# GpSimd makes one of four shifted exp copies and the normalising multiplications in place of VectorE

## The chip, the cores and the metric

The kernel runs on one NeuronCore of one Trainium2 chip. The metric is the time of one execution on the device, in microseconds (us). Executions of one kernel mostly agree within a per cent. "Faster" or "slower" needs a difference of over 2%.

The engines in the profile are PE (TensorE matmuls), PEld (TensorE weight loads), DVE (VectorE), ACT (ScalarE), POOL (GpSimd) and SP (SyncE, which issues DMAs here). The granted clock is the share of its full speed that TensorE was given, as the profile reports it. In the experiments a ratio compares the fast runs of one kernel with those of the kernel before in the same rounds, on the same chip; it is given as the measuring program recorded it, and is not quite the ratio of the medians that stand beside it.

## The reference

One transformer block: 2048 tokens, width 512, 32 heads of 16 columns, a gated FFN of width 1792, with shifts and scales made from a conditioning vector.

```python
h = layernorm(x) * (1 + ca) + sa
q, k, v = split(h @ wqkv)                       # 32 heads, Dh = 16
p = softmax(q @ k.T * Dh ** -0.5)
x = x + ga * ((p @ v) @ wo)
h = layernorm(x) * (1 + cb) + sb
x = x + gb * ((gelu(h @ w_gate) * (h @ w_up)) @ w_down)
```

What matters here: 32 x 2048 x 2048 scores have to go through an exponential. That is the dominant work of the kernel.

## The kernel before

A Python program decides the order of instructions on each engine, when the kernel is built, with a timing model of its own. Every engine then runs its list in order, and semaphores keep the dependences. All operations go through a few helpers, so a whole class of instructions shows one line in the profile: 309 is every matmul, 322 every ScalarE activation, 334 every `tensor_scalar`, 326 every `tensor_tensor`, 343 every copy.

Scores go to six PSUM banks in two groups of three. TensorE fills a group, ScalarE exponentiates it to bf16 in SBUF (`E`) while TensorE fills the other group. ScalarE cannot keep up with all blocks, so VectorE takes some. For a "quad" of four score blocks VectorE takes the third bank of the group, one block at a time, and writes an integer that is the bit pattern of a rough exponential:

```python
# (cut) in stream(): one step of the score loop
self.qk([(seq[m], k) for m, k in items])                       # TensorE: fill three banks
self.act(self.E[:, e0:e0 + n, :], self.scp[:, s0:s0 + n, :], ACT.Exp, scale=EXP_SCALE)
if g is not None:                                              # VectorE has the third bank
    j = quad["j"]
    kq = self.kq[quad["k"]]
    self.ts("dve", kq[:, 512 * j:512 * j + 512].bitcast(U16), self.scp[:, s0 + n, :], 128 / OCT, SHIFT_C,
            ALU.mult, ALU.add)
    ...
    if j == 3:
        quad["ready"].append((0, [kq[:, 512 * x:512 * x + 512] for x in range(4)]))
        for i in range(NS):                                    # NS = 4 shifted copies
            self.shift_task(quad, i)
```

One such block is too rough. The quad is multiplied with V, and four copies of it, each with a constant added to the bit pattern, with four scaled versions of V; the sum is accurate enough. Each copy is one instruction of 2048 columns of uint16, SBUF to SBUF, and one more group of matmuls reads it:

```python
def shift_task(self, q, i):
    def f():
        s = self.sq_free[0]
        self.ts("dve", self.sq[s].bitcast(U16), self.kq[q["k"]].bitcast(U16), float(SHIFT[i]), None, ALU.add)
        if self.probing is None:
            self.sq_free.pop(0)
            ...
            q["ready"].append((i + 1, [self.sq[s][:, 512 * x:512 * x + 512] for x in range(4)]))
    self.task([f], ("shift", q["rnd"][0]), lambda: bool(self.sq_free))
```

When a unit (eight of them make a set of query rows) is finished, its output is multiplied by reciprocals of the row sums, which come back from a round trip through DRAM:

```python
def fin2():
    c = OCOL[sets[0]]
    self.tt("dve", self.onorm[:, qd, c:c + W], osb, rb, ALU.mult)
```

The model of time that the scheduler uses has a line for GpSimd. `short(t)` in the same class inserts filler matmuls, whose results nobody reads, wherever the model finds TensorE idle and its recent activity below a mark (`FILL`).

```python
def cost(self, eng, out, ins, kind):
    ...
    if eng == "act":
        return n * 0.833 + (60 if ps else 92)
    if eng == "pool":
        return n * 3.0 + 100
```

The softmax here doesn't subtract the row's maximum and nothing guards it: scores larger than these inputs give would overflow.

## Time and profile before

| | before |
|---|---|
| time, median of 2 runs | 906.15 us (906.06 to 906.24) |
| span of the profiled run | 904.5 us |
| mean granted TensorE clock | 0.981 |
| busy, whole span: ScalarE / TensorE / VectorE / GpSimd | 841.9 / 817.2 / 687.5 / 3.7 us |

The first view is the table of stretches, for 102 to 780 us, which is from the first to the last shifted copy. Each engine's busy time is followed by its number of instructions in brackets; then come the granted clock, the DMA share and GB/s.

```profile
core 0: us, PE busy (x) PEld busy (x) DVE busy (x) ACT busy (x) POOL busy (x), PEclk, DMA share, GB/s
102.00:780.00 678.00, 638.02 (x9029) 199.85 (x9021) 570.82 (x996) 674.16 (x594) 0.00 (x0) 1.00 0.16 44
```

ScalarE is busy 674.2 of 678 us. It is the limit, and it is idle for 4 us. VectorE has 107 us of idle time there and GpSimd does nothing.

In the tile names, `dreg` and `mreg` are SBUF regions that hold quads and their copies, `ps_sc` is the banks of scores, `ps_pv` the bank of p @ v, which `osb` takes over, and `ps_mi` a bank for other products; `wreg` and `hreg` hold intermediate values of the FFN and other work. The groups of instructions, with shapes kept apart, give the price of each piece: columns are line, engine, operation, output<-input, shape, count | busy us, mean ns | idle us before, and who ended it.

```profile
L334 DVE TENSOR_SCALAR dreg<-ps_sc 128x512 uint16<-128x512 f32 x188 | 129.5, 690 | 36.0 <-PE ps_sc L309 34.0
L334 DVE TENSOR_SCALAR mreg<-dreg 128x2048 uint16<-128x2048 uint16 x188 | 123.1, 682 | 2.8 <-PE ps_pv L309 2.8
L334 DVE TENSOR_SCALAR mreg<-ps_sc 128x512 uint16<-128x512 f32 x92 | 63.0, 689 | 16.0 <-PE ps_sc L309 15.0
L334 DVE TENSOR_SCALAR mreg<-mreg 128x2048 uint16<-128x2048 uint16 x92 | 60.3, 684 | 0.9 <-PE ps_pv L309 0.9
L326 DVE TENSOR_TENSOR wreg<-wreg 128x1024 bf16<-128x1024 bf16 x42 | 28.3, 683 | 0.2
```

There are 188 + 92 = 280 evictions from PSUM at 690 ns, so 70 quads, and 280 copies at 683 ns. A copy handles four times as many columns as an eviction in the same time. The last line is a product of two SBUF tensors.

The waits of ScalarE and TensorE in the same stretch (engine and tile <- who ended the wait: us in total, times, longest us):

```profile
ACT E L322 <- PE ps_sc L309: 2.8, 9, 0.7
```
```profile
PE ps_sc L309 <- ACT E L322: 20.0, 61, 0.8
PE ps_mi L309 <- DVE wreg L339: 5.0, 8, 1.2
PE ps_mi L309 <- DVE wreg L343: 2.6, 5, 0.8
PE ps_mi L309 <- DVE kmo L334: 1.7, 5, 0.5
PE ps_pv L309 <- DVE mreg L334: 1.4, 6, 0.5
```

ScalarE almost never waits for scores. TensorE waits mostly for ScalarE to free a bank, which is as it should be with ScalarE as the limit.

### The profile page before, as it was taken

The page shows a single profiled execution, that of the slowest core. Times are in us where ns is not written, and L with a number is a line of the kernel's source. Part 1 is how long each engine was busy: PE and PEld are TensorE (multiplying, and loading weights), DVE is VectorE, ACT ScalarE, POOL GpSimd, SP SyncE. Part 2 cuts the span into 40 slices and gives each one's busy share as a digit, 9 for nine tenths or more (in the row PEclk, how much of TensorE's full clock was granted, in tenths as well). Part 3 has the DMA queues.
Part 4 walks back from the last instruction along what each step waited for, and adds up shares of the span by engine and source line. Part 5 has one row for each costly group of instructions (what it writes and reads, how often), then busy time and mean ns, then how long its engine had stood idle before and what let it go on. Part 6 is the DMA issues. An engine that isn't in the chain of part 4 may idle for free.

```text
span 904.5 us, 29537 instructions
## 1 busy us (share of the span) xinstructions
PE 817.2 (90%) x13408; PEld 288.4 (32%) x13408; DVE 687.5 (76%) x1303; ACT 841.9 (93%) x747; POOL 3.7 (0%) x11
## 2 busy tenths in 40 slices
PE   5898899999999999999999999999998899888885
PEld 2333232322232222222222222223432333345454
DVE  4854678988899889999898899888866744545372
ACT  3999899999999999999999999999999999978871
POOL 1000000000000000000000000000000000000000
PEclk7999899999999999999999999999999999979999
DMA  9000000000102111211003211110122221553400
GB/s 302 3 26 15 15 3 26 4 27 2 26 14 72 37 49 49 52 45 38 26 2 99 61 42 53 49 31 26 27 79 72 78 66 53 152 150 104 112 7 15
DMA packets 74935, 47.76 MB, mean 53 GB/s; under 512 B 17693, under 2 KB 70618, under 8 KB 74810
## 3 DMA queue, kind: packets, MB, share of 16 engines
q1 hardware_dynamic: 72426, 44.30, 16.9%
q8 instruction: 105, 1.72, 0.8%
q10 hardware_dynamic: 2384, 1.57, 0.6%
q14 instruction: 20, 0.16, 0.1%
HBM read 43.25 MB, written 2.61 MB: 51 GB/s over the span
## 4 chain that ended last, share of the span: by engine, by line
ACT 51%; PE 31%; DMA 7%; DVE 7%; SPq 3%; issue 2%; DVEq 0%
ACT E L322 49%; PE ps_mi L309 13%; PE ps_sc L309 12%; PE ps_pv L309 6%; DMA scr_rec<-rden 3%; SPq L372 3%; ACT wreg L322 2%; DMA mreg<-in_B_w_gate_dram 1%; DVE mreg L334 1%; DMA mreg<-in_w_mod_dram 1%; DVE wreg L326 1%; DVE wreg L339 1%; DVE wreg L343 1%; DMA rb<-scr_rec 1%; DMA mreg<-in_B_w_down_dram 1%
## 5 line engine op out<-in xcount | busy, mean ns | idle before, releaser
L322 ACT ACTIVATE E<-ps_sc 128x1536 bf16<-128x1536 f32 (+2 forms) x698 | 811.6, 1318 | 35.2 <-PE ps_sc L309 33.9
L309 PE MATMUL ps_sc<-qT,kmo 32*128 32x512 bf16 (+2 forms) x1408 | 183.8, 328 | 10.8 <-ACT E L322 7.5
L309 PE MATMUL ps_sc<-qT,kme 32*128 32x512 bf16 (+2 forms) x1344 | 178.0, 333 | 14.4 <-ACT E L322 12.1
L309 PE MATMUL ps_pv<-E,vaug 128*17 128x512 bf16 (+2 forms) x2380 | 175.7, 323 | 3.5 <-ACT E L322 1.7
L334 DVE TENSOR_SCALAR dreg<-ps_sc 128x512 uint16<-128x512 f32 x188 | 129.5, 690 | 36.0 <-PE ps_sc L309 34.0
L309 PE MATMUL ps_mi<-wreg,mreg 128*32 128x512 bf16 (+2 forms) x1920 | 124.1, 355 | 17.4 <-DVE wreg L339 5.4
L334 DVE TENSOR_SCALAR mreg<-dreg 128x2048 uint16<-128x2048 uint16 x188 | 123.1, 682 | 2.8 <-PE ps_pv L309 2.8
L309 PE MATMUL ps_pv<-mreg,vs 128*17 128x512 bf16 (+1 forms) x1232 | 98.4, 361 | 1.9 <-DVE mreg L334 1.4
L309 PEld LDWEIGHTS ps_sc<-qT,kme 32*128 32x128 bf16 x1344 | 46.6, 91 | 133.1 <-ACT E L322 92.6
L309 PEld LDWEIGHTS ps_sc<-qT,kmo 32*128 32x128 bf16 x1408 | 49.2, 93 | 121.7 <-ACT E L322 83.4
L309 PEld LDWEIGHTS ps_pv<-E,vaug 128*17 128x17 bf16 x2380 | 53.3, 89 | 91.3 <-issue 61.1
L334 DVE TENSOR_SCALAR mreg<-ps_sc 128x512 uint16<-128x512 f32 x92 | 63.0, 689 | 16.0 <-PE ps_sc L309 15.0
L309 PEld LDWEIGHTS ps_mi<-wreg,mreg 128*32 128x32 bf16 x1920 | 42.8, 98 | 73.9 <-issue 26.0
L334 DVE TENSOR_SCALAR mreg<-mreg 128x2048 uint16<-128x2048 uint16 x92 | 60.3, 684 | 0.9 <-PE ps_pv L309 0.9
L343 DVE CAST wreg<-ps_mi 128x512 bf16<-128x512 f32 x51 | 35.0, 686 | 23.9 <-PE ps_mi L309 23.3
L339 DVE SCALAR_TENSOR_TENSOR wreg<-wreg,ps_mi 128x512 bf16<-128x512 bf16 x51 | 34.9, 683 | 18.4 <-PE ps_mi L309 14.4
L309 PE MATMUL ps_sc<-xs,ident 128*32 128x512 bf16 x352 | 31.6, 401 | 11.4 <-ACT E L322 10.6
L309 PE MATMUL ps_mi<-hreg,wreg 128*32 128x512 bf16 x480 | 39.9, 391 | 0.7 <-DVE vaug L343 0.5
L309 PEld LDWEIGHTS ps_pv<-mreg,vs 128*17 128x17 bf16 x1232 | 29.4, 89 | 34.5 <-DVE mreg L334 16.6
L326 DVE TENSOR_TENSOR onorm<-osb,rb 128x512 bf16<-128x512 f32 (+2 forms) x43 | 23.6, 549 | 19.8 <-DMA rb<-scr_rec 19.6
L309 PE MATMUL ps_mi<-mreg,hreg 128*32 128x512 bf16 x448 | 36.5, 384 | 0.2 <-DMA mreg<-in_B_w_down_dram 0.2
L309 PE MATMUL ps_mi<-wo,onorm 128*32 128x512 bf16 x480 | 36.0, 387 | 0.7 <-DVE wreg L326 0.5
(136 smaller groups left out, 560.5 us busy)
## 6 DMA issues: line engine op xcount, KB each, us to landing
mreg<-in_B_w_up_dram SPq DMA_DIRECT2D x32, 256.0 KB, 3.4
mreg<-in_B_w_gate_dram SPq DMA_DIRECT2D x28, 256.0 KB, 3.3
rb<-scr_rec SPq DMA_DIRECT2D x96, 64.0 KB, 2.0
mreg<-in_B_w_down_dram SPq DMA_DIRECT2D x16, 256.0 KB, 2.8
dreg<-in_B_w_down_dram SPq DMA_DIRECT2D x12, 256.0 KB, 4.5
mreg<-in_w_mod_dram SPq DMA_DIRECT2D x1, 2048.0 KB, 14.3
out_dram<-xs SPq DMA_DIRECT2D x16, 128.0 KB, 1.8
rb<-scr_rec SPq DMA_DIRECT2D x52, 32.0 KB, 1.8
```

Of the source, the lines that this page charges most:

```text
L309: return self.rec("pe", lambda e: e.matmul(out, lhsT, rhs, start=start, stop=stop, tile_position=tp), [lhsT, rhs], [out], cost=(n, int(rhs ...
L322: return self.rec("act", lambda e: e.activation(out, in_, func, scale=scale, **kw), rd, wr, cost=self.cost("act", out, [in_], "act"))
L326: return self.rec(eng, lambda e: e.tensor_tensor(out, a, b, op), [a, b], [out], cost=self.cost(eng, out, [a, b], "tt"))
L334: return self.rec(eng, lambda e: e.tensor_scalar(out, a, s1, s2, **kw), rd, [out], cost=self.cost(eng, out, [a], "ts"))
L339: return self.rec("dve", lambda e: e.scalar_tensor_tensor(out, a, s, b, op0=op0, op1=op1), rd, [out], cost=self.cost("dve", out, [a, b], " ...
L343: return self.rec(eng, lambda e: e.tensor_copy(out, in_), [in_], [out], cost=self.cost(eng, out, [in_], "ts"))
L372: return e.dma_start(out, in_)
```

## The change

The intent: VectorE is the third busiest engine in the stretch, after ScalarE and TensorE, and GpSimd is free. Let GpSimd make the last of each quad's four copies, and the multiplications by reciprocals. With VectorE lighter, the scheduler may give it more exps. The time model of GpSimd is adjusted (`n` is the number of columns), and the list of ready copies is handled by identity, as copies now become ready out of order.

```diff
         if eng == "pool":
-            return n * 3.0 + 100
+            return n * (1.2 if kind == "ts" and n == 2048 else 2.2) + 200
@@
             else:
-                q["ready"].pop(0)
+                q["ready"].remove((i, src))
@@
             s = self.sq_free[0]
-            self.ts("dve", self.sq[s].bitcast(U16), self.kq[q["k"]].bitcast(U16), float(SHIFT[i]), None, ALU.add)
+            kq = self.kq[q["k"]].bitcast(U16)
+            if i == NS - 1:
+                self.ts("pool", self.sq[s].bitcast(U16), kq, 1.0, float(SHIFT[i]), ALU.mult, ALU.add)
+            else:
+                self.ts("dve", self.sq[s].bitcast(U16), kq, float(SHIFT[i]), None, ALU.add)
@@
         def fin2():
             c = OCOL[sets[0]]
-            self.tt("dve", self.onorm[:, qd, c:c + W], osb, rb, ALU.mult)
+            self.tt("pool", self.onorm[:, qd, c:c + W], osb, rb, ALU.mult)
```

## The prediction

> **What bounds it now.** ScalarE. In the table of stretches, from 102 to 780 us (first to last shifted copy on VectorE), ScalarE is busy 674.2 of 678 us, VectorE 570.8, TensorE 638.0, GpSimd 0. The chain of waits there is nearly all exps. The groups by line show 280 PSUM evictions (690 ns) and 280 shifted copies (683 ns) on VectorE, so 70 quads; ScalarE's 1536-wide exp averages 1508 ns, the 1024-wide 1096 ns, so a block taken off ScalarE is worth 412 ns.
>
> **What the change does.** By the order of instructions VectorE loses 61 copies (280 to 219) and 39 of 43 normalisations (24 of 682 ns, 13 of 424 ns, 2 small) and gains 12 evictions; GpSimd gets 73 copies and 39 multiplications; there are 73 quads, so 12 exps shrink from 1536 to 1024 columns.
> - ScalarE: 12 x 0.412 = 5 us less, on the critical path: the whole direct gain. ScalarE idles only 4 us in the stretch, so freeing VectorE earns nothing more.
> - VectorE: about 55 us less busy (61 x 0.683, plus 22, minus 12 x 0.69), off the critical path.
> - GpSimd: the trace has no comparable instruction. From the rates in the Trainium skill ("GPSIMD Engine Reference", Performance versus the Vector engine) I estimate 2.0 to 2.7 us for a copy and 1.2 us for a 512-wide multiplication: 180 to 240 us in all.
>
> **What it may cost.** The Trainium skill ("SBUF — State Buffer", Who interferes with whom) says that GpSimd shares its SBUF ports with VectorE by a lock held for a whole instruction, against VectorE operations in a two-port mode or with two SBUF inputs. The copies (2048 elements in 683 ns) must be in such a mode; GELU multiplications and residual additions have two inputs. Between first and last copy some 370 of VectorE's 913 instructions are of these kinds. The trace before cannot show the lock. If it holds, VectorE reaches a blocked instruction after one or two others on average, and waits 1 to 2 us. Estimate: 73 x 1.4 plus 39 x 0.5, about 120 us of waiting against 55 us relieved: VectorE occupied about 94% of the stretch instead of 84%, in lumps longer than an exp. Evictions behind a blocked copy come late, so the score bank, TensorE's next scores and ScalarE come late. Second path: GpSimd's copy, delayed by VectorE's, comes after the place the scheduler gave its consumer, and TensorE, in order, waits. I guess 20 to 60 us of new ScalarE idle time; without the lock, none.
>
> **Prediction: 930 us**, 8 in 10 between 897 and 978. Faster by over 2%: 0.04; within 2%: 0.39; slower by over 2%: 0.57.
>
> **What would show it.** Right: (a) ScalarE busy 5 us less, but its idle time from 102 to 780 us up from 4 to 25 us or more, released by TensorE's scores, which waited for VectorE's evictions or GpSimd's copies; (b) VectorE's 2048-wide copies and SBUF multiplications longer than before (or gaps before them without a semaphore's cause), while PSUM evictions keep 690 ns; (c) GpSimd busy 180 to 260 us; (d) TensorE waiting for GpSimd before the matmuls of mreg with vs. Wrong: VectorE's copies keep 683 ns beside a running GpSimd and ScalarE stays 99% busy: then about 900 us.
>
> **What would make it wrong.** The lock may be finer than an instruction; or evictions may run far enough ahead of ScalarE to swallow the lumps: then 898 to 908. Or a GpSimd copy takes over 4 us and holds the port half of the time: then over 978.

## The result and the profile after

| | before | after |
|---|---|---|
| time, median of 2 runs | 906.15 us | 972.9 us (972.61 to 973.2) |
| ratio, 95% interval | | 1.0746 (1.0697 to 1.0795) |
| span of the profiled run | 904.5 us | 971.5 us |
| ScalarE busy / idle, whole span | 841.9 / 62.6 us | 848.2 / 123.3 us |
| TensorE busy, mean granted clock | 817.2 us, 0.981 | 849.5 us, 0.938 |
| VectorE busy | 687.5 us | 716.5 us |
| GpSimd busy | 3.7 us | 201.6 us |

The kernel became 7.5% slower. The stretch with quads now ends at about 850 us:

```profile
102.00:850.00 748.00, 670.40 (x8975) 199.69 (x8967) 597.74 (x910) 676.96 (x591) 190.53 (x104) 0.93 0.14 39
```

ScalarE's idle time there is 748 - 677 = 71 us, where it was 4. No engine is the limit now: TensorE is busy 90% of the stretch, ScalarE 91%, VectorE 80%. The granted clock in the stretch fell from 1.00 to 0.93.

The groups of the kernel after:

```profile
L334 DVE TENSOR_SCALAR mreg<-dreg 128x2048 uint16<-128x2048 uint16 x147 | 141.3, 988 | 4.1 <-PE ps_pv L309 4.0
L334 DVE TENSOR_SCALAR dreg<-ps_sc 128x512 uint16<-128x512 f32 x196 | 133.3, 686 | 55.3 <-PE ps_sc L309 54.0
L334 DVE TENSOR_SCALAR mreg<-mreg 128x2048 uint16<-128x2048 uint16 x72 | 66.8, 946 | 0.4 <-PE ps_pv L309 0.3
L334 DVE TENSOR_SCALAR mreg<-ps_sc 128x512 uint16<-128x512 f32 x96 | 65.5, 687 | 21.2 <-PE ps_sc L309 20.6
L326 DVE TENSOR_TENSOR wreg<-wreg 128x1024 bf16<-128x1024 bf16 x42 | 33.1, 791 | 0.3
L334 POOL TENSOR_SCALAR mreg<-dreg 128x2048 uint16<-128x2048 uint16 x49 | 100.9, 2058 | 331.4 <-PE ps_pv L309 291.9 <-PE ps_sc L309 12.0 <-DVE rden L346 11.2
L334 POOL TENSOR_SCALAR mreg<-mreg 128x2048 uint16<-128x2048 uint16 x24 | 50.1, 2087 | 95.8 <-PE ps_pv L309 82.0 <-DVE mreg L334 9.6 <-PE ps_sc L309 4.2
L326 POOL TENSOR_TENSOR onorm<-osb,rb 128x512 bf16<-128x512 f32 x24 | 35.5, 1478 | 84.3 <-DMA rb<-scr_rec 55.4 <-PE ps_mi L309 28.8
```

VectorE's own 2048-column copies, the same instruction as before, went from 683 ns to 988 and 946 ns, and its products of two SBUF tensors from 683 to 791 ns. Its evictions from PSUM kept 686 ns. So something lengthens only some of VectorE's instructions. The waiting is inside the instruction's busy time: the list of waits does not know of it.

The waits in the stretch, the same views as before:

```profile
ACT E L322 <- PE ps_sc L309: 65.5, 92, 3.2
```
```profile
PE ps_pv L309 <- DVE mreg L334: 24.4, 35, 1.6
PE ps_sc L309 <- ACT E L322: 13.1, 37, 0.9
PE ps_mi L309 <- DVE wreg L339: 10.8, 16, 2.6
PE ps_pv L309 <- DVE osb L343: 9.9, 6, 3.5
PE ps_mi L309 <- DVE wreg L343: 6.2, 8, 2.9
```

ScalarE now waits 65.5 us for scores, and TensorE, which makes the scores and runs in order, waits for VectorE. It never waits for GpSimd: no such line is in the list.

One place shows the whole course. The timelines of GpSimd, VectorE, TensorE and ScalarE of the kernel after around 305 us (start us, duration us, instruction; in brackets the idle time before it):

```profile
299.57 2.02 POOL L334 TENSOR_SCALAR mreg<-dreg 128x2048 uint16<-128x2048 uint16 x1 [10.66 <-PE ps_pv L309]
...
304.63 2.12 POOL L334 TENSOR_SCALAR mreg<-mreg 128x2048 uint16<-128x2048 uint16 x1 [1.38 <-PE ps_pv L309]
```
```profile
299.75 2.39 DVE L334 TENSOR_SCALAR mreg<-dreg 128x2048 uint16<-128x2048 uint16 x1
...
304.31 0.69 DVE L334 TENSOR_SCALAR mreg<-mreg 128x2048 uint16<-128x2048 uint16 x1
304.91 1.87 DVE L334 TENSOR_SCALAR rstd<-nwx 128x4 int32<-128x4 int32 x1
306.68 0.68 DVE L334 TENSOR_SCALAR mreg<-mreg 128x2048 uint16<-128x2048 uint16 x1
...
307.35 0.68 DVE L343 COPY osb<-ps_pv 128x512 f32<-128x512 f32 x1
```
```profile
305.00 0.39 PE L309 MATMUL ps_sc<-qT,kme 32*128 32x512 bf16 x3
308.09 0.61 PE L309 MATMUL ps_pv<-mreg,vaug 128*17 128x512 bf16 x4 [2.69 <-DVE osb L343]
...
309.05 0.61 PE L309 MATMUL ps_sc<-qT,kme 32*128 32x512 bf16 x3
```
```profile
309.70 1.02 ACT L322 ACTIVATE E<-ps_sc 128x1024 bf16<-128x1024 f32 x1 [2.61 <-PE ps_sc L309]
```

GpSimd's copy begins at 304.63. VectorE's next instruction works on four columns and takes 0.16 us elsewhere; here it takes 1.87 us and ends when GpSimd does. The copy that empties the output bank, three instructions later on VectorE, is late by as much. TensorE stands 2.69 us for that bank, with the next scores behind it in its list, and ScalarE then has nothing to do for 2.61 us. When TensorE resumes, the same group of three score matmuls takes 0.61 us where it took 0.39: its granted clock is 0.59 from 308 to 312 us, where it was 1.00 from 300 to 306.

To count such waits I took, from the trace, every VectorE instruction that lasts more than 150 ns over the median of its group in the kernel before. There are 70, with 79 us in all; the mean is 1.13 us.

The same count, over this kernel and nine of the experiments below (all but `short_hold`, `thin_fill` and the paired ones), shows which instructions wait. Of VectorE's instructions that began with at least 0.2 us left of a running GpSimd copy or multiplication, none of 749 with an operand in PSUM was lengthened, and none of 65 with operands in SBUF that are reciprocals or batch-norm statistics. Of 593 `tensor_scalar` and two-input operations within SBUF 569 were; 18 of the other 24 began with less than 0.3 us of GpSimd's instruction left, so that too little was added to count. Of all 570 long instructions only one began at another time.

### The profile page after: what moved, and what is told of

Read it like the earlier page. It is cut to its first block, busy times and chain, and to the rows that moved or that the text cites. A ratio compares the mean times of both kernels' runs of the same rounds, so it can differ in the third digit from the quotient of the medians.

```text
span 971.5 us, 29629 instructions
## 1 busy us (share of the span) xinstructions
PE 849.5 (87%) x13436; PEld 289.1 (30%) x13436; DVE 716.5 (74%) x1215; ACT 848.2 (87%) x747; POOL 201.6 (21%) x123
## 3 DMA queue, kind: packets, MB, share of 16 engines
HBM read 43.25 MB, written 2.61 MB: 47 GB/s over the span
## 4 chain that ended last, share of the span: by engine, by line
PE 43%; DVE 28%; ACT 24%; issue 3%; DMA 2%; SPq 1%; DVEq 0%
ACT E L322 22%; PE ps_sc L309 17%; PE ps_mi L309 15%; DVE mreg L334 14%; PE ps_pv L309 10%; DVE dreg L334 4%; DVE wreg L326 2%; ACT wreg L322 1%; DVE wreg L343 1%; DVE wreg L339 1%; DMA mreg<-in_w_mod_dram 1%; DVE wreg L334 1%; DMA mreg<-in_B_w_up_dram 1%; SPq L372 1%; DVE xs L326 1%
## 5 line engine op out<-in xcount | busy, mean ns | idle before, releaser
L322 ACT ACTIVATE E<-ps_sc 128x1536 bf16<-128x1536 f32 (+2 forms) x698 | 817.2, 1272 | 94.7 <-PE ps_sc L309 92.0
L309 PE MATMUL ps_sc<-qT,kmo 32*128 32x512 bf16 (+2 forms) x1408 | 188.9, 335 | 10.9 <-ACT E L322 7.8
L309 PE MATMUL ps_sc<-qT,kme 32*128 32x512 bf16 (+2 forms) x1344 | 184.5, 349 | 10.9 <-ACT E L322 8.9
L334 POOL TENSOR_SCALAR mreg<-dreg 128x2048 uint16<-128x2048 uint16 x49 | 100.9, 2058 | 331.4 <-PE ps_pv L309 291.9
L334 DVE TENSOR_SCALAR mreg<-dreg 128x2048 uint16<-128x2048 uint16 x147 | 141.3, 988 | 4.1 <-PE ps_pv L309 4.0
L309 PE MATMUL ps_pv<-mreg,vs 128*17 128x512 bf16 (+1 forms) x1280 | 108.3, 384 | 25.7 <-DVE mreg L334 25.7
L326 POOL TENSOR_TENSOR onorm<-osb,rb 128x512 bf16<-128x512 f32 (+2 forms) x39 | 47.6, 1221 | 253.1 <-DMA rb<-scr_rec 224.2
L334 DVE TENSOR_SCALAR mreg<-ps_sc 128x512 uint16<-128x512 f32 x96 | 65.5, 687 | 21.2 <-PE ps_sc L309 20.6
L334 POOL TENSOR_SCALAR mreg<-mreg 128x2048 uint16<-128x2048 uint16 x24 | 50.1, 2087 | 95.8 <-PE ps_pv L309 82.0
L334 DVE TENSOR_SCALAR mreg<-mreg 128x2048 uint16<-128x2048 uint16 x72 | 66.8, 946 | 0.4 <-PE ps_pv L309 0.3
L326 DVE TENSOR_TENSOR wreg<-wreg 128x1024 bf16<-128x1024 bf16 (+1 forms) x60 | 41.1, 687 | 0.8
```

What stands on the lines that cost most here:

```text
L309: return self.rec("pe", lambda e: e.matmul(out, lhsT, rhs, start=start, stop=stop, tile_position=tp), [lhsT, rhs], [out], cost=(n, int(rhs ...
L322: return self.rec("act", lambda e: e.activation(out, in_, func, scale=scale, **kw), rd, wr, cost=self.cost("act", out, [in_], "act"))
L326: return self.rec(eng, lambda e: e.tensor_tensor(out, a, b, op), [a, b], [out], cost=self.cost(eng, out, [a, b], "tt"))
L334: return self.rec(eng, lambda e: e.tensor_scalar(out, a, s1, s2, **kw), rd, [out], cost=self.cost(eng, out, [a], "ts"))
```

## The experiments

Theory L (lock): GpSimd and VectorE exclude each other at an SBUF port for whole instructions; VectorE's waits are the cause and all else follows. Theory O (order): the scheduler's new order, or GpSimd's copies coming too late for TensorE, is the cause. Theory C (clock): TensorE's falling clock multiplies a small loss. 14 kernels were run. All gave results within the tolerance of the reference, among them `short_hold`, which leaves most of the normalised attention output at zero: passing says little about that part. One execution of `copies_only` was slow and is left out here. A ratio within 2% of 1 counts as the same speed by the rule above; `pieces_copies` and `paired_idle` are unclear, as their intervals reach past 2%.

| run | time (us) | before, same rounds | ratio, 95% interval | clock, profiled run |
|---|---|---|---|---|
| short_hold | 898.1 | 907.6 | 0.990 (0.987 to 0.994) | 0.990 |
| load_only | 958.2 | 907.6 | 1.057 (1.053 to 1.062) | 0.963 |
| copies_only | 955.0 | 907.6 | 1.056 (1.048 to 1.063) | 0.963 |
| mults_only | 911.1 | 907.6 | 1.006 (1.002 to 1.010) | 0.987 |
| load_half | 917.4 | 905.6 | 1.013 (1.008 to 1.017) | 0.979 |
| load_spread | 911.7 | 906.9 | 1.006 (1.002 to 1.011) | 0.983 |
| thin_fill | 915.1 | 905.6 | 1.013 (1.007 to 1.019) | 0.949 |
| load_thin | 982.3 | 911.8 | 1.077 (1.072 to 1.082) | 0.905 |
| pieces | 919.0 | 905.6 | 1.015 (1.010 to 1.020) | 0.966 |
| pieces_copies | 929.2 | 911.8 | 1.020 (1.015 to 1.025) | 0.972 |
| aware | 941.0 | 905.6 | 1.039 (1.033 to 1.044) | 0.976 |
| paired | 951.5 | 911.8 | 1.044 (1.040 to 1.048) | 0.978 |
| paired_idle | 922.1 | 906.9 | 1.016 (1.010 to 1.022) | 0.970 |
| paired_some | 905.7 | 906.9 | 0.999 (0.993 to 1.005) | 0.987 |

### short_hold: the changed order, without the long GpSimd instructions

```diff
-                self.ts("pool", self.sq[s].bitcast(U16), kq, 1.0, float(SHIFT[i]), ALU.mult, ALU.add)
+                o_ = self.sq[s].bitcast(U16)
+                self.rec("pool", lambda e: e.tensor_scalar(o_[:, 0:2], kq[:, 0:2], 1.0, ...), [kq], [o_], cost=...)
```

The same is done to the multiplication; two memsets in the prologue keep uninitialised memory from being read (and leave the output at zero where the shortened multiplications do not write). Dependences are recorded as if the whole tile were written.

> The changed kernel's order of instructions on TensorE, VectorE, ScalarE and the DMA queue, unchanged; but each GpSimd copy and multiplication touches two columns instead of all (a wrong result on purpose). Lock theory (GpSimd's hold of the port makes VectorE wait, all else follows): VectorE's 2048-wide copies back at 683 ns, granted clock back at about 0.98, time 895 to 908. Order theory (the new order of instructions is worse by itself): stays within 2% of 973. This run alone does not tell the lock from copies that come too late for TensorE, as both are gone.

Measured: 898.1 us, 1% less than before, which is within the 2% but clear of 1 in its interval. The new order alone is not worse: ScalarE's busy time falls from 841.9 to 836.1 us, and VectorE's copies are back at 685 and 682 ns. Theory O in its first form falls. The 898 us is also about what this order of instructions could give if GpSimd cost nothing.

### load_only: the order before, with GpSimd copies that nobody reads

```diff
+                if i == NS - 1 and g_ is not None:          # g_: a part of qT that is dead at the time
+                    src = self.km[0][:, 0, :].rearrange("p (a b) -> p a b", a=4).bitcast(U16)
+                    dst, pace = self.qT[:, :, 512 * g_:512 * g_ + 512].bitcast(U16), self.sq[s][:, 0:2]
+                    self.rec("pool", lambda e: e.tensor_scalar(dst, src, 1.0, 3.0, op0=ALU.mult, op1=ALU.add),
+                             [src, pace], [dst], cost=2000)
```

The order on TensorE, ScalarE, VectorE and the DMA queue was compared in the built programs: it is that of the kernel before, instruction by instruction. No reader waits for these 64 copies.

> The kernel before, the same order on every other engine; GpSimd in addition makes 64 copies of 2048 columns that nobody reads, each released by VectorE's fourth copy of a quad. The result stays right. Lock theory: VectorE's 2048-wide copies lengthen to a mean of 850 ns or more, about 50 to 70 us of waiting, granted clock falls to 0.96 or lower, time 940 to 985. Theories of order or of copies that come too late for their reader: 904 to 910, as nothing waits for these copies.

Measured: 958.2 us. The groups:

```profile
L334 DVE TENSOR_SCALAR mreg<-dreg 128x2048 uint16<-128x2048 uint16 x188 | 148.8, 818 | 2.5 <-PE ps_pv L309 2.4
L334 DVE TENSOR_SCALAR dreg<-ps_sc 128x512 uint16<-128x512 f32 x188 | 127.8, 686 | 34.3 <-PE ps_sc L309 33.4
L1376 POOL TENSOR_SCALAR qT<-kme 128x2048 uint16<-128x2048 uint16 x64 | 130.6, 2041 | 578.5 <-DVE mreg L334 522.1 <-PE ps_mi L309 40.3 <-DVE nwt L326 16.1
```

The copies lengthen (818 ns, a little below the 850 expected), the evictions do not, and the time rises by 51 us. With VectorE's list unchanged, its busy time grew from 687.5 to 739.8 us, by 52 us, and the time by 51 us. That the two are so near is not a transfer one to one: ScalarE is idle for 27 us from the start of these waits until 2.5 us after them, of 42 us by which its idle time rose; its busy time rose by another 9 us. Theory O falls in its second form too. GpSimd's bare presence at the port is sufficient for a loss of this kind.

### copies_only and mults_only: one part of the change alone

```diff
-            self.tt("pool", self.onorm[:, qd, c:c + W], osb, rb, ALU.mult)
+            self.tt("dve", self.onorm[:, qd, c:c + W], osb, rb, ALU.mult)
```
```diff
-            if i == NS - 1:
+            if False:
```

> The changed kernel with the multiplications back on VectorE: 73 or so copies on GpSimd, 151 of the 199 us that GpSimd held. Lock theory: most of the loss stays, 945 to 970. If the multiplications (48 us, two SBUF inputs) did most harm: below 925.

> The changed kernel with all copies back on VectorE: GpSimd makes only the multiplications, about 48 us of holding. Lock theory: 908 to 925, a quarter of the loss or less. If the multiplications did most harm: over 940.

Measured: 955.0 and 911.1 us. The copies do most of the harm. Both are also orders of their own, with 74 and 70 quads. The multiplications, a quarter of GpSimd's time, cost 4 us alone; VectorE has 16 waits with 12.8 us in that run, and the 43 - 4 multiplications that left it were worth nothing, as ScalarE is the limit.

### load_half and load_spread: shorter holds

`load_half` is `load_only` with 1024 columns in each copy. `load_spread` makes four copies of 512 columns per quad, one behind each eviction:

```diff
+                        src = self.km[0][:, 0, 512 * j:512 * j + 512].bitcast(U16)
+                        dst = self.qT[:, j, 512 * g_:512 * g_ + 512].bitcast(U16)
+                        self.rec("pool", lambda e, src=src, dst=dst: e.tensor_scalar(dst, src, 1.0, 3.0, ...),
+                                 [src, kq[:, 512 * j:512 * j + 2]], [dst], cost=600)
```

> As the run with 64 unread GpSimd copies on the order of the kernel before, but each of 1024 columns instead of 2048, so about 1.1 us instead of 2.04. If the loss is VectorE's waiting time passed on one to one (52 us of added VectorE busy time cost 51 us in the full load): added VectorE busy time 12 to 30 us and the time up by about the same, 918 to 938. If a stall costs by its number and not by its length: 945 or more.

> The kernel before, the same order on every other engine; GpSimd makes 257 unread copies of 512 columns, each released by one of VectorE's evictions, so it holds the port longer in all than in the full load (about 155 us against 131) but never longer than 0.6 us. If only the part of a wait beyond a slack of about 0.8 us reaches ScalarE: 907 to 920, even with 25 us or more of added VectorE busy time. If the sum of waits is passed on one to one: the time rises by as much as VectorE's busy time does, 930 or more when that is 25 us.

All three load runs have the kernel before's order on the other engines. The waits are counted in the traces as above; the last column is ScalarE's idle time from the start of such an instruction until 2.5 us after its end, averaged over the waits of that length.

| run | GpSimd instructions | GpSimd busy | VectorE's waits | span against 904.5 | waits by length: number, ScalarE idle after |
|---|---|---|---|---|---|
| load_spread | 257 x 512 columns | 195 us | 32, 12.6 us | +4.8 us | under 0.5 us: 32, 0.03 us |
| load_half | 64 x 1024 | 75 us | 37, 21.3 us | +11.8 us | under 0.5: 21, 0.02; 0.5 to 1: 16, 0.25 |
| load_only | 64 x 2048 | 131 us | 48, 58.6 us | +51.2 us | under 0.5: 3, 0.00; 0.5 to 1: 10, 0.14; 1 to 1.5: 21, 0.47; 1.5 to 2: 14, 1.13 |

`load_spread` keeps GpSimd busiest of the three and costs least:

```profile
L1299 POOL TENSOR_SCALAR qT<-kme 128x512 uint16<-128x512 uint16 x257 | 195.3, 761 | 462.3 <-DVE dreg L334 336.0 <-DVE mreg L334 123.7 <-DVE nwx L334 1.6
```

Two things follow. First, VectorE waits less in sum, 12.6 us instead of the 25 that I had thought possible; the expectation's test case did not quite arise. `load_half`, at 917.4 us, ended just below its forecast of 918 to 938. Second, the length of a wait decides what is passed on: a wait under 0.5 us leaves ScalarE 0.03 us idle, one of 1.5 to 2 us leaves 1.13 us. There is a slack of several tenths of a microsecond per wait: in `load_only` the waits of 0.5 to 1, 1 to 1.5 and 1.5 to 2 us have means of 0.79, 1.24 and 1.69 us, which is 0.65, 0.77 and 0.56 us more than what ScalarE loses. The slack is not a constant of the kernel: waits of 1.5 to 2 us leave ScalarE 1.16 us idle in the kernel after, 0.64 us in `aware`. Nor is it the length alone that differs in `load_spread`, whose copies start at other places; `load_half` changes the length alone, and halving it cuts the added time from 51 to 12 us. A likely reason for the slack is that a bank group has the length of one exp of the other group (0.92 us for a 1024-wide one back to back) to be emptied and refilled; that reason is argued, the table is measured.

### thin_fill and load_thin: the clock

The filler matmuls keep their places in the order but touch 2 columns instead of 512, so TensorE has less to do and its activity is lower. `load_thin` adds `load_only`'s copies.

```diff
-        return self.rec("pe", lambda e: e.matmul(out, lhsT, rhs, ...
+        ro, rr = (out[:, 0:2], rhs[:, 0:2]) if rhs is getattr(self, "fill_rhs", None) else (out, rhs)
+        return self.rec("pe", lambda e: e.matmul(ro, lhsT, rr, ...
```

> The kernel before, the same order, no GpSimd work; its filler matmuls (128 groups of four, 512 columns, results unused) touch 2 columns instead of 512, so TensorE has less to do and is less active. Theory that the granted clock is an amplifier of its own: the mean granted clock falls from 0.98 to 0.94 or lower and the time rises to 925 or more with VectorE's copies still at 683 ns. Theory that the clock only mirrors the waiting and costs little: 900 to 912, whatever the clock.

> The 64 unread GpSimd copies of 2048 columns on the order of the kernel before, together with the thin fillers (2 of 512 columns). Alone the copies cost 51 us and the thin fillers 9. If TensorE's falling clock amplifies a stall, less activity to begin with makes it worse: over 985, clock below 0.92. If the stalls pass on directly and the clock adds little: the sum, 955 to 975.

Measured: 915.1 and 982.3 us; both lie between the two theories' figures. A clock of 0.949 instead of 0.981 costs about 1.3% with no wait on VectorE at all. Together with the load the ratio is 1.077, where the product of the two alone is 1.057 x 1.013 = 1.071. So the clock costs something. That it amplifies a stall is not shown: the 0.6% lies within the intervals of the three runs, though the clock, 0.905, fell as far as the amplifier's theory had it. It is not the main term: `load_only` lost 5.7% with the clock at 0.963. What share of the 7.5% the clock has in the changed kernel, where it fell to 0.938, was not isolated; from `thin_fill` (0.032 less clock for 1.3%, some 12 us) the 0.043 less of the changed kernel would be about 16 us, so I estimate 10 to 20 of the 67 us.

### pieces and pieces_copies: the change with short GpSimd instructions

```diff
-                self.ts("pool", self.sq[s].bitcast(U16), kq, 1.0, float(SHIFT[i]), ALU.mult, ALU.add)
+                for x in range(4):
+                    self.ts("pool", self.sq[s][:, 512 * x:512 * x + 512].bitcast(U16), kq[:, 512 * x:512 * x + 512],
+                            1.0, float(SHIFT[i]), ALU.mult, ALU.add)
```

> The changed kernel with each GpSimd copy in four instructions of 512 columns, about 0.6 us each. If the length of one hold decides how long VectorE stands: waiting per blocked instruction at most about 0.6 us unless GpSimd takes the port again first, VectorE's copies at a mean below 850 ns, time 915 to 945. If only the share of time in which GpSimd holds the port matters, or GpSimd's pieces follow each other without letting VectorE in: 965 or more.

> As the run with the copies in four pieces, but the multiplications on VectorE. Port theory: a few us less than that run's 919: 908 to 918, VectorE's copies at 740 to 800 ns. If pairing does nothing, the paired run is the same as this one.

Measured: 919.0 us for `pieces`. Cutting each copy in four, and setting the scheduler's cost of it, takes back some 54 us of the 67 (the quads stay 73, but the order is another one, with 564 filler matmuls instead of 492) although GpSimd is busy longer (262.8 us instead of 201.6). VectorE's waits are 90 with 38 us in sum, 81 of them under 0.5 us. Such short waits are followed by 0.17 us of ScalarE's idle time here, against 0.03 us in `load_spread`, so they are not free in every order. `pieces_copies`, with the multiplications back on VectorE, should have been a little faster and was not: 929.2 us, where the kernel before took 911.8 in the same rounds, a ratio of 1.020 against 1.015, with intervals that overlap. VectorE's copies, at 814 ns in the mean, were also above the 740 to 800 expected. It makes 75 quads instead of 73, so it is another schedule; this miss was not followed up.

### aware: a scheduler that knows the lock

In its time model, a VectorE instruction with both operands in SBUF starts after GpSimd's hold, and the reverse; GpSimd's rate is set to the measured one.

```diff
+            if eng == "pool" and cost > 600:
+                t = max(t, self.dve_two)
+                self.hold = t, t + cost
+            elif eng == "dve" and self.two:
+                if self.hold[0] - 60 <= t < self.hold[1]:
+                    t = self.hold[1]
+                self.dve_two = t + cost
```

> The changed kernel with a scheduler whose timing model knows the exclusive port (a two-port or two-input VectorE operation starts after GpSimd's hold, and the reverse) and GpSimd's measured rate. It makes 68 quads instead of 73. If the loss came from an order that did not reckon with the waits: under 925. If the waits themselves cost whatever the order: 940 to 970.

Measured: 941.0 us with 68 quads. VectorE still waits 73 us. Reckoning with the waits, without avoiding them, regains less than half. Yet 73 us of waits cost 35 us here and 79 us cost 67 in the kernel after: the order has a say in how much of a wait is passed on.

### paired, paired_idle, paired_some: GpSimd only beside VectorE's single-port work

The scheduler issues a 512-column piece only behind the VectorE instruction that stands just before one that reads PSUM, and a semaphore holds it there. Multiplications stay on VectorE.

```diff
+        if eng == "dve" and dma is None and not self.two and cost >= 590 and self.jobs and op.seq > 1:
+            start = op.t1 - 92 - cost                    # (cut)
+            if self.free["pool"] <= start + 100 and self.probe(lambda: self.piece(job, 0)) <= start + 100:
+                self.piece(job, op.seq - 1)              # waits for VectorE's instruction before this one
```

In `paired_idle` a copy goes to GpSimd only if none waits there, and pieces are also issued where the model finds VectorE idle. `paired_some` keeps copies on VectorE when the unit has four or fewer of its plain rounds left:

```diff
-            if i == NS - 1 and len(self.jobs) < 1:
+            if i == NS - 1 and len(self.jobs) < 1 and self.plain[q["rnd"][0]] > 4:
```

> GpSimd makes the fourth copy of each of 70 quads, in four pieces of 512 columns; 249 of the 280 pieces wait for the VectorE instruction just before one that reads PSUM, so that a piece of about 0.6 us runs while VectorE runs that single-port instruction of 0.69 us; multiplications stay on VectorE. Port theory: GpSimd is busy some 170 us without harm; VectorE's 2048-wide copies at a mean below 730 ns, time 895 to 912. If any GpSimd activity beside VectorE costs (not only two-port or two-input operations): 920 or more.

> As the paired run, but a copy goes to GpSimd only when none is waiting there (60 of 71 quads), and pieces are also issued when the scheduler sees VectorE idle or after 8 us. If the paired run lost by late copies alone: VectorE's copies below 720 ns, ScalarE's longest wait for scores under 6 us and 895 to 915. If not: 930 or more.

> As paired_idle, but copies near the end of a unit stay on VectorE: 44 of 70 quads on GpSimd. If late copies are what is left: 895 to 910 and not slower than paired_idle.

The first kernel missed its time (951.5 us, which alone would speak for the rival forecast of 920 or more) but not its mechanism. GpSimd was busy 176 us, and VectorE's copies stayed at 690 and 688 ns. Its loss is another one, and the likely reason is that pieces that wait for suitable places come late; ScalarE's longest wait is now 9.9 us.

```profile
ACT E L360 <- PE ps_sc L347: 75.0, 60, 9.9
```

At that place, 699 to 709 us, four pieces of one copy run at 697.5, 699.5, 703.7 and 704.8 us; the scheduler, knowing that nothing can be done, has put 68 filler matmuls there, and the matmuls that read mreg start at 706.1. In the whole trace TensorE waits only 0.5 us for GpSimd itself, so the lateness would be built into the order. With copies kept from coming late the time falls step by step, 922.1 us (between the two forecasts of 895 to 915 and 930 or more) and 905.7 us. Each step also changes the order and sends fewer copies to GpSimd, so late copies are argued as the cause, not isolated. In the last kernel the pieces run undisturbed at 618 ns and VectorE's copies keep their length:

```profile
L266 POOL TENSOR_SCALAR mreg<-dreg 128x512 uint16<-128x512 uint16 x112 | 68.5, 618 | 434.1 <-DVE mreg L374 143.0 <-PE ps_sc L347 89.4 <-DVE kmo L374 49.3
L266 POOL TENSOR_SCALAR mreg<-mreg 128x512 uint16<-128x512 uint16 x64 | 39.3, 617 | 176.7 <-DVE mreg L374 93.0 <-PE ps_sc L347 52.8 <-PE ps_mi L347 13.8
```
```profile
L374 DVE TENSOR_SCALAR mreg<-dreg 128x2048 uint16<-128x2048 uint16 x160 | 105.7, 688 | 6.1 <-PE ps_pv L347 5.9
L374 DVE TENSOR_SCALAR mreg<-mreg 128x2048 uint16<-128x2048 uint16 x76 | 50.8, 690 | 2.7 <-PE ps_pv L347 2.7
```

So GpSimd's work beside VectorE's single-port instructions does no harm, which is the lock theory's last test. It also does no measurable good: with 44 of 70 fourth copies on GpSimd the time is that of the kernel before (0.999, interval 0.993 to 1.005). No version that beats both kernels was found; `short_hold` says that with the order of the kernel after about 1% was to be had.

## Why the prediction was right and where it was wrong

Right:

- *The limit and the direct gain.* ScalarE was the limit, and a block taken from it saves, back to back, 1346 - 919 = 427 ns in the trace (412 had been read from the means). Without GpSimd's holds the gain is there (`short_hold`: ScalarE's busy time 5.8 us less).
- *The lock and its signature.* The Trainium skill, "SBUF — State Buffer", Who interferes with whom, describes an exclusive port held for an instruction, against VectorE's two-port modes and its instructions with two SBUF inputs. Traces agree: copies 683 to 988 ns, products of two SBUF tensors 683 to 791 ns, evictions from PSUM unchanged at 686 ns, the count of 570 waits above, and the causal runs `load_only` (5.7% slower from copies that nobody reads) and `short_hold`. Points (b) and (c) of the forecast were met: GpSimd was busy 201.6 us.
- *The direction*, and the range: 972.9 us is inside 897 to 978, near its end.

Wrong, and it was the size:

- *The failing step* is the term "I guess 20 to 60 us of new ScalarE idle time", together with "ScalarE: 12 x 0.412 = 5 us less". The prediction's 930 is 906 - 5 + 29; the 29 seems to weigh the case of a lock with that of none, which the prediction does not spell out. With the lock taken as certain and the middle of the guess it would have been 906 - 5 + 40 = 941. Measured: ScalarE's idle time rose by 60.7 us and its busy time by 6.3 us, together the 67.0 us between the two spans. So the idle time came out at the top of the guess and twice what the 930 holds, and the 5 us of gain turned into a loss.
- *How much of a wait is passed on.* I had estimated 120 us of VectorE's waiting and guessed that a sixth to a half of it would reach ScalarE. The trace has 70 waits with 79 us, fewer and less than estimated, but most of it got through: `short_hold` and the kernel after, with the same order, differ by 72 us in VectorE's busy time and by 77 us in span (a fallen clock included). VectorE's 107 us of idle time gave no protection. What protects is the slack at the single wait, and the load runs put that at several tenths of a microsecond; a wait for a GpSimd copy of 2 us can go far beyond it.
- *ScalarE's busy time.* An exp that follows another without a gap adds 919 ns (1024 columns) or 1346 ns (1536); after a gap it adds 1024 or 1451 ns, 105 ns more. In the kernel after 142 of these exps start after a gap of over 50 ns, before it was 40. 102 x 0.105 = 10.7 us, less the 5.1 us of twelve blocks, is close to the 6 us found. Idle gaps carry their own small price, which the forecast did not have.
- *TensorE's clock.* It was not in the forecast. TensorE's busy time rose by 32 us although it had fewer filler matmuls; part of the 67 us is that (10 to 20 us by estimate).
- *The second path.* TensorE waiting for a late GpSimd copy, point (d), does not occur in the kernel after. What TensorE waits for are VectorE's own copies (24.4 us in the stretch, 1.4 before) and its eviction of the output bank. Late GpSimd copies became a loss, as far as can be told, only in the paired kernels.
- *VectorE "occupied 94%".* It was 80% of a longer stretch. The share of busy time was the wrong measure: no engine was full, and the time was lost in a chain of short stalls.

## What to carry to other kernels

Before giving idle GpSimd a part of VectorE's work, count how many of VectorE's instructions beside it use two ports or two SBUF inputs; each GpSimd instruction may then hold one of them for its whole length. Charge the waits by their length against the slack at the place where they fall, not by the idle share of the waiting engine; if the work must go to GpSimd, cut it into instructions shorter than that slack and put them beside instructions that read PSUM. Here that only brought back the time of the kernel before. Look for a port wait in the mean durations of unchanged instructions, as it is not in the list of waits.

## What the Trainium skill lacked or had wrong

- "SBUF — State Buffer", Who interferes with whom: the lock is as described, but the page does not say that in a profile the wait appears as a longer busy time of the blocked instruction (683 to 988 ns here; 0.16 to 1.87 us for an instruction on four columns) and in no list of waits.
- The same page, the summary for kernel authors, advises to schedule whichever engine is off the critical path. VectorE was not the limit, with 107 us idle in 678, and the change still cost 67 us. No page gives shorter GpSimd instructions as a remedy for these waits: 64 of 2048 columns cost 51 us, 64 of 1024 columns 12 us, 257 of 512 columns, started at other places, 5 us.
- "GPSIMD Engine Reference", Performance versus the Vector engine, gives about 1.03 cycles at 1.2 GHz for each element of a light one-input body but no figure for the fixed cost of an instruction. The runs agree with the rate to some 3% and add the rest: 2048 uint16 columns of multiply and add took 1.897 us undisturbed and 512 took 0.62 us, which is 0.83 ns per column and 0.19 us fixed.
- "TensorE: Matmul & The Clock Gate" has no figure for what thinner filler matmuls cost a kernel that another engine limits: here the mean granted clock went from 0.981 to 0.949 and the time up by 1.3%.
